# A fused attention and gated-MLP block on one core: the first stage written out as one order of steps, with the first chunk's maxima in it

## The chip, the core and the metric

The kernel runs on one core of a Trainium2 chip. The metric is the device time of one execution in microseconds (us). The core has five engines that run side by side, each working through its own instructions in order: TensorE (PE; its weight loads are listed apart as PEld), VectorE (DVE), ScalarE (ACT), GpSimd (POOL) and SyncE (SP). SP does nothing here but issue DMAs: it too works in order, so a DMA that has to wait for something holds up all DMAs behind it on SP. A few DMAs are issued by POOL instead.

## The reference

From one input of 2048 rows by 512 columns the kernel computes a parallel sum: the input, plus multi-head attention with 32 heads of width 16, plus a gated MLP with a matrix product along the sequence. Both branches read the same layer-normed input.

```python
x = A_x
xn = _layernorm(x, axis=-1)
return x + _A_ref(xn, A_wqkv, A_wo) + _B_ref(xn, B_w_in, B_w_sp, B_b_sp, B_w_out)

# _A_ref: q, k, v = split(x @ wqkv); softmax(q k^T / 4) v, heads joined; @ wo
# _B_ref: z = gelu(x @ w_in); z1, z2 = halves, z2 layer-normed
#         g = w_sp @ z2 + b_sp;  (z1 * g) @ w_out
```

## The kernel before

**Numbers.** Every product but scores, maxima and values is made of three passes over operands that are split into a rounded high part and a low part (`mm3` L242, `split` L238: ACT copies the high part out of PSUM, DVE subtracts it from PSUM to give the low part). Weights that come from memory are split the same way.

**First stage (L1034 to L1078, a fixed order of instructions).** The rows come in four groups g = 0..3 of 512 rows. For each group: `norm_x` takes the mean and variance of each 128-row tile on DVE (L339, L340), the root on ACT (L342), two small operations on DVE (L343, L344), and the scaling of the tile on POOL (L348). `turn_x` transposes the group on PE (L354, four chunks c of 128 columns) and splits each chunk into `xnT[g, c]`. `qk_first` computes q and k of the first eight heads for the group (24 products of 512 columns, L243 to L245), splits them, stores them through SP to memory (`qscr`, `kscr`: two DMAs each, 512 KB and 256 KB), and `load_stacks` reads the rows of the first two heads back into `qst[0]`, `kst[0]` (four DMAs of 96 KB, issued by SP after the stores have landed). V is made in tiles of 128 rows: the first four (EARLY = 4) here, by `v_tile`, between the q and k of the groups. The first two weight pieces (`wqk0`) are loaded twice: by SP as they are, and by POOL's queue rounded to the high part (L260), so that DVE only subtracts (L266). V's weights are split on POOL (L268, L269). The transposed groups 0 and 1 are stored to memory from POOL's queue (L162, eight DMAs of 512 KB).

**Steady stage (from L1079).** Here a planner in Python writes the order. It holds modelled times of PE, ACT, DVE and POOL in `T`, and at each step emits one of:
- S, a score tile (L1149: two products, then one exp of 128x1024 on ACT);
- M, a maximum tile (L1163: two products, then one maximum over 128x1024 on DVE, L868). Sixteen of them give the 512 query rows of one chunk (for two heads); `max_fin` joins them on DVE (L879 to L885), sends them through memory (`mscr`) into two rows of `qst`, and only then the chunk's scores can start (`maxready`);
- D, one dense slot (L1208: two products on the two halves of the array, 0.23 us of PE): all the rest, in a fixed queue: the other twelve V tiles (`v_rest`, 144 slots), q and k of the other heads (288), the MLP's parts, the two output products;
- V, a burst of 32 value products (L1246), which needs the exps of eight S, and, in the first two bursts, the V tiles of rows 0 to 1023 and 1024 to 2047;
- a filler (L1222), products of zeros while nothing else can run.

One cycle is 8 S, 9 or 7 M in turn, up to 24 D and one V (`ORDER`); there are 16 pairs of heads, four chunks each, two cycles a chunk: 128 cycles. A dense unit is 24 slots (18 for the attention's output product), after which its two PSUM banks `dps` are copied out (`yield "e"`, then `"q"`). If a unit ends after more than 11 slots of a cycle, the dense queue is held until that cycle's V (`hold`), so units and cycles keep step. `mx_ok` lets M start at planner time 7.0 (FIRST), and at most 30 of them run ahead before the first scores (LEAD).

## Time and profile before

| | us |
|---|---|
| median of 3 runs | 1860.66 |
| lowest and highest run | 1859.05, 1863.14 |
| the profiled execution | 1862.6 |
| its span, first to last instruction | 1860.4 |
| PE busy | 1811.4 (97%) |
| DVE busy | 1441.5 (77%) |
| ACT busy | 1189.1 (64%) |
| POOL busy | 722.3 (39%) |
| DMA | 306 MB, mean 165 GB/s |

All times below are us from the start of the span. A row of the **timeline** is: start, length, engine, line of the kernel, operation, what it writes `<-` what it reads, partitions x elements, count, and in brackets how long the engine sat idle before it and what ended that. `SPq` is a DMA issue on SP; its start is when SP got to issue it. A row of the **windows** view is a stretch, its length, the busy time of each engine (and how many instructions touch the stretch), PE's granted clock (1.00 is 2.4 GHz, 0.50 is 1.2 GHz), the DMA engines' share and GB/s; where only one line is asked for, only that line's busy time stands. A row of the **groups** view is line, engine, operation, shapes, count | total busy us, mean ns of one | idle time before. Products are pipelined: a row of PE of 0.39 us is followed by the next after 0.23.

### The profile page before, as it was taken

Reading aid. Unit: us, or ns where it says so; the run is one execution under the profiler, and the core shown is the slowest. Engines: PE = TensorE matmul, PEld = TensorE weight load, DVE = VectorE, ACT = ScalarE, POOL = GpSimd, SP = SyncE. Lnnn points to the kernel's source line nnn. Section 1 sums busy time; section 2 is a strip of 40 time slices with the busy share of each in tenths; the row PEclk is TensorE's granted clock in tenths of the full one; section 3 lists DMA queues with packets and bytes.
Section 4 is the critical chain, followed back from the end, with each engine's and each line's share of the span. In section 5 each row is a group of like instructions: output and inputs, shape, how many; then the busy total and the mean of one; then the engine's idle time right before and its main releaser. Section 6 shows DMA issues by size and latency. Waiting matters only on the chain.

```text
span 1860.4 us, 38081 instructions
## 1 busy us (share of the span) xinstructions
PE 1811.4 (97%) x14804; PEld 1099.5 (59%) x14804; DVE 1441.5 (77%) x1677; ACT 1189.1 (64%) x1292; POOL 722.3 (39%) x808
## 2 busy tenths in 40 slices
...
GB/s 227 283 98 282 277 242 87 127 92 110 136 215 134 106 113 204 156 156 162 217 166 199 157 179 206 158 150 155 193 168 182 174 185 143 129 182 149 112 78 90
DMA packets 212124, 306.14 MB, mean 165 GB/s; under 512 B 36816, under 2 KB 108048, under 8 KB 209056
## 3 DMA queue, kind: packets, MB, share of 16 engines
...
q8 instruction: 116, 1.90, 0.4%
...
## 4 chain that ended last, share of the span: by engine, by line
PE 84%; DVE 6%; DMA 4%; POOL 3%; issue 2%; ACT 1%; SPq 1%; DVEq 0%; POOLq 0%; ACTq 0%
PE dps L1208 34%; PE sl L1246 23%; PE sl L1149 13%; PE sl L1163 12%; DVE mm L868 4%; PE dps L1222 1%; DMA zs<-z2scr 1%; DMA kscr<-qkhl 1%; SPq L132 1%; ACT pf L76 1%; POOL wsp L291 1%; DMA wsp_15r<-in_w_spT 0%; POOL wsp L289 0%; DMA wsp_0r<-in_w_spT 0%; DMA qst<-mscr 0%
## 5 line engine op out<-in xcount | busy, mean ns | idle before, releaser
L868 DVE TENSOR_REDUCE mm<-sl 128x2 f32<-128x1024 f32 x1024 | 1224.4, 1222 | 203.7 <-PE sl L1163 199.1
L76 ACT ACTIVATE pf<-sl 128x1024 f32<-128x1024 f32 x1024 | 1041.1, 1026 | 338.8 <-PE sl L1149 297.3
L1246 PE MATMUL sl<-pf,vall 128*32 128x512 f32 x4096 | 468.4, 598 | 0.7 <-DVE mm L868 0.4
L1149 PE MATMUL sl<-qst,kst 50*128 50x512 f32 x2048 | 437.8, 419 | 11.1 <-DVE mm L868 4.3
L1163 PE MATMUL sl<-kst,qst 48*128 48x512 f32 x2048 | 424.0, 406 | 4.5 <-DVE mm L868 2.2
L1208 PE MATMUL dps<-wsp,zs 64*128 64x512 f32 x2352 | 382.1, 393 | 2.6 <-DMA zs<-z2scr 2.6
L1149 PEld LDWEIGHTS sl<-qst,kst 50*128 50x128 f32 x2048 | 195.8, 184 | 218.4 <-issue 79.3
L1246 PEld LDWEIGHTS sl<-pf,vall 128*32 128x32 f32 x4096 | 120.5, 110 | 271.2 <-issue 237.4
L1163 PEld LDWEIGHTS sl<-kst,qst 48*128 48x128 f32 x2048 | 196.5, 185 | 105.9 <-ACT pf L76 55.3
L1208 PEld LDWEIGHTS dps<-wsp,zs 64*128 64x128 f32 x2352 | 229.3, 187 | 40.4 <-DMA zs<-z2scr 4.1
L76 ACT ACTIVATE e<-sl 128x512 f32<-128x512 f32 x64 | 38.3, 598 | 208.0 <-PE sl L1246 198.0
L1266 DVE TENSOR_TENSOR e<-sl,e 128x512 f32<-128x512 f32 x64 | 44.3, 692 | 136.4 <-PE sl L1246 70.2
L774 POOL TENSOR_TENSOR hhl<-z1i,hhl 128x512 fp32r<-128x512 f32 x28 | 35.9, 1292 | 275.8 <-ACT hhl L76 275.8
L1208 PE MATMUL dps<-w,xt 64*128 64x448 f32 x768 | 110.6, 368 | 1.5
L1208 PE MATMUL dps<-wout,hp 64*128 64x512 f32 x672 | 110.3, 392 | 0.0
L915 POOL TENSOR_TENSOR ob<-ob 128x512 f32<-128x512 f32 (+1 forms) x16 | 20.5, 1284 | 201.5 <-DMA ob<-rscr 186.6
L1208 PEld LDWEIGHTS dps<-w,xt 64*128 64x128 f32 x768 | 73.9, 186 | 16.0 <-issue 7.8
L1208 PEld LDWEIGHTS dps<-wout,hp 64*128 64x128 f32 x672 | 65.5, 187 | 9.1
L911 POOL TENSOR_TENSOR ob<-ob 128x512 f32<-128x512 f32 (+1 forms) x16 | 21.0, 1315 | 117.5 <-DMA ob<-escr 117.5
L441 POOL TENSOR_TENSOR qkhl<-qr,qkhl 128x512 fp32r<-128x512 f32 x24 | 30.4, 1286 | 69.9 <-ACT qkhl L76 65.8
L1208 PE MATMUL dps<-wf,zs 64*128 64x512 f32 x336 | 55.5, 392 | 0.1
L1208 PE MATMUL dps<-xnT,wqk 64*128 64x512 f32 x288 | 47.7, 395 | 1.1 <-ACT vall L76 0.4
...
## 6 DMA issues: line engine op xcount, KB each, us to landing
zs<-z2scr SPq DMA_DIRECT2D x192, 256.0 KB
...
```

What stands on the lines that cost most here:

```text
L76: return nc.scalar.activation(out, in_, func, **kw)
L132: nc.sync.dma_start(raw(dst), raw(src))
L441: nc.gpsimd.tensor_sub(hl[:, 1, :], raw_, hl[:, 0, :].bitcast(F32))
L774: nc.gpsimd.tensor_sub(hl[:, 1, :], z1, hl[:, 0, :].bitcast(F32))
L868: nc.vector.tensor_reduce(mmax[g][:, :, t, kc], sl[k], AX.X, ALU.max)
L911: nc.gpsimd.tensor_add(both_[rows, 0, :], both_[rows, 0, :], both_[rows, 1, :])
L915: nc.gpsimd.tensor_mul(both_[rows, 0, :], both_[rows, 0, :], both_[rows, 1, :])
L1149: nc.tensor.matmul(sl[k][:, j, :], kst[p % 2][rows, kt * P:(kt + 1) * P], qst[p % 2][rows, c * 512:(c + 1) * 512], start=True, stop=True)
L1163: nc.tensor.matmul(sl[k][:, j, :], qst[p % 2][rows, tt * P:(tt + 1) * P], kst[p % 2][rows, kc * 512:(kc + 1) * 512], start=True, stop=True)
L1208: nc.tensor.matmul(dps[:, bank, :w], lhs, rhs, start=go, stop=stop)
L1246: nc.tensor.matmul(sl[k][cols:cols + VW, 0, :], vpack(kt + r, 2 * p + j), pf[:, j * 512:(j + 1) * 512], start=n == n_pv, stop=n == n_pv + ...
L1266: nc.vector.tensor_add(e, sl[k][:, 0, :], e)
```

## The change

The first stage becomes one written order. `STEPS` is a string of words, `First.step` emits each word's instructions, and so it fixes the order on each engine; digits are group and chunk (or half, or tile), `*` picks another engine. S: statistics of two tiles, R: root and the small operations, N: scaling (`*`: the second tile on ACT), T: transposes, E: split of a chunk, Q: the twelve products of q (second digit 0) or k (1), F: its split and store (`*`: ACT copies twice and POOL subtracts), L: load back into the stacks, Z: store of a transposed chunk, now on SP, VH and VL: high and low parts of V's weights (`*`: POOL; else ACT and DVE), V and VE: a V tile and its copy, WH and WL: high and low parts of the first weights (ACT, DVE), B: the bias row, M and X: a maximum tile of the first chunk (first digit the 512 keys, second the tile of queries) and its maximum on DVE.

- All sixteen maxima of the first chunk stand in it, so the planner starts with `n_mx = 16` and with `max_fin(0)` at once; FIRST goes.
- The four early V tiles stand behind nearly all q and k.
- 22 idle products (`WARM`) on zeros are put in front of PE's work.
- POOL's second load of the first weights goes; ACT rounds them.
- The store of ones (`cscr`) moves behind the last load of x, the memsets of V's ones move to the front of POOL.
- In the steady stage: `v_out` copies bank 1 on DVE instead of ACT, the hold needs more than 8 slots instead of 11 and is off until all V tiles are done, the planner starts with ACT at 0.6 and DVE at 2.0.

```diff
-FIRST = 7.0
...
+WARM = 22
+STEPS = (
+    "S00 S01 R00 WH0 N00 WL0 R01 S10 N01* T01 S11 WH1 T03 E03 T00 E01 R10 T02 WL1 E02 E00 R11 N10 N11* Q00 T13 T12 "
+    "T11 F00* S20 VH1* S21 E13 R21 E12 Q01 Z13 VH3* T10 N21* S30 R20 E11 E10 Q11 VL1* R30 N20 F01* B VH0 Z03 N30* "
+    "T20 S31 E20 R31 T23 Z02 Z11 L0 F11 Z10 Z01 E23 N31* Q10 F10 T32 T21 T22 T30 E32 E22 E21 Q20 VH2 L1 T31 VL3 E30 "
+    "T33 Q21 VL0 F20 E31 VL2 M02 E33 M00 Q31 X02 F21 M13 M10 L2 X00 Q30 X13 F31 M03 M01 X10 X03 F30 V3 M22 M12 Z00 "
+    "X01 M23 VE3 X22 Z12 V0 VE0 X12 M21 X23 M20 X21 L3 M11 V1 X20 M32 M30 X11 M31 X32 X31 VE1 V2 X30 M33 X33 VE2 "
+)
...
     def v_out(t, bank):
-        yield "A", ta(512)
-        act(vhead[:, t, :, :DH], dps[:, bank, :].rearrange("p (h d) -> p h d", d=DH), AF.Copy)
+        src = dps[:, bank, :].rearrange("p (h d) -> p h d", d=DH)
+        if bank:
+            yield "D", td(512)
+            nc.vector.tensor_copy(vhead[:, t, :, :DH], src)
+        else:
+            yield "A", ta(512)
+            act(vhead[:, t, :, :DH], src, AF.Copy)
         rel()
...
+    class First:
+
+        def __init__(self, w0r, w0, wvr, wv, braw):
+            self.w0r, self.w0, self.wvr, self.wv, self.braw = w0r, w0, wvr, wv, braw
+            self.acc, self.rs, self.mv, self.came, self.split_, self.turn = {}, {}, {}, [], [], 0
+
+        def step(self, word):
+            name = word.rstrip("*0123456789").lower()
+            getattr(self, name)(*map(int, word[len(name):].rstrip("*")), other=word.endswith("*"))
+
+        def take(self, *key):
+            self.turn += 1
+            self.acc[key] = (dps, *sl)[self.turn % 4]
+            return self.acc[key]
+
+        def s(self, g, h, other):
+            self.mv[g, h] = mv = sm.tile([P, 2, 2], F32, tag="mv", name=f"mv{g}_{h}", bufs=4)
+            for i in range(2):
+                st = sm.tile([P, 6], F32, tag="bst", name=f"bst{g}_{h}_{i}", bufs=4)
+                nc.vector.bn_stats(st, xs[g, 2 * h + i])
+                nc.vector.bn_aggr(mv[:, i, :], st)
+
+        def r(self, g, h, other):
+            mv = self.mv[g, h]
+            self.rs[g, h] = rs = sm.tile([P, 2, 2], F32, tag="rs", name=f"rs{g}_{h}", bufs=4)
+            nc.scalar.activation(rs[:, 0, :], mv[:, :, 1], AF.Sqrt, bias=epst)
+            nc.vector.reciprocal(rs[:, 0, :], rs[:, 0, :])
+            nc.vector.scalar_tensor_tensor(rs[:, 1, :], mv[:, :, 0], -1.0, rs[:, 0, :], ALU.mult, ALU.mult)
+
+        def n(self, g, h, other):
+            rs = self.rs[g, h]
+            for i in range(2):
+                x = xs[g, 2 * h + i]
+                if i and other:
+                    act(x, x, AF.Identity, bias=rs[:, 1, i:i + 1], scale=rs[:, 0, i:i + 1])
+                else:
+                    nc.gpsimd.tensor_scalar(x, x, rs[:, 0, i:i + 1], rs[:, 1, i:i + 1], ALU.mult, ALU.add)
+
+        def t(self, g, c, other):
+            acc = self.take("t", g, c)
+            for i in range(4):
+                nc.tensor.transpose(acc[:, 0, i * P:(i + 1) * P], xs[g, i][:, c * P:(c + 1) * P], ident)
+
+        def e(self, g, c, other):
+            xnT[g, c] = t = piece(f"xnT{g}_{c}")
+            split(t[:, 0, :], t[:, 1, :], self.acc["t", g, c][:, 0, :])
+            self.came.append((g, c))
+
+        def z(self, g, c, other):
+            move(xscr[g][c], xnT[g, c])
+
+        def wh(self, a, other):
+            act(self.w0[a][:, 0, :], self.w0r[a], AF.Copy)
+
+        def wl(self, a, other):
+            nc.vector.tensor_sub(self.w0[a][:, 1, :], self.w0r[a], self.w0[a][:, 0, :].bitcast(F32))
+
+        def q(self, g, a, other):
+            acc = self.take("q", g, a)
+            cs = [c for h, c in self.came if h == g]
+            for c in cs:
+                t, w = xnT[g, c], self.w0[a]
+                mm3(acc[:, 0, :], w[:, 0, c * P:(c + 1) * P], w[:, 1, c * P:(c + 1) * P], t[:, 0, :], t[:, 1, :], c == cs[0], c == cs[-1])
+
+        def f(self, g, a, other):
+            acc = self.acc["q", g, a][:, 0, :]
+            hl = hilo(f"qkhl0_{a}_{g}")
+            if other:
+                raw_ = t512(f"qr0_{a}_{g}")
+                act(raw_, acc, AF.Copy)
+                act(hl[:, 0, :], raw_, AF.Copy)
+                nc.gpsimd.tensor_sub(hl[:, 1, :], raw_, hl[:, 0, :].bitcast(F32))
+            else:
+                split(hl[:, 0, :], hl[:, 1, :], acc)
+            qk_store((qscr, kscr)[a][0], QK[a], hl, slice(g * 512, (g + 1) * 512), True)
+
+        def l(self, g, other):
+            load_stacks(0, slice(g * 512, (g + 1) * 512))
+
+        def b(self, other):
+            bhl = hilo("bhl")[0:16, :, 0:P]
+            nc.vector.tensor_copy(bhl[:, 0, :], self.braw)
+            nc.vector.tensor_sub(bhl[:, 1, :], self.braw, bhl[:, 0, :].bitcast(F32))
+            for a in range(2):
+                move(bsplit[a:a + 1, :], bhl[:, a, :])
+
+        def vh(self, c, other):
+            t, rw = self.wv[c], self.wvr[c]
+            if other:
+                nc.gpsimd.tensor_copy(t[:, 0, :], rw)
+            else:
+                act(t[:, 0, :], rw, AF.Copy)
+
+        def vl(self, c, other):
+            t, rw = self.wv[c], self.wvr[c]
+            (nc.gpsimd if other else nc.vector).tensor_sub(t[:, 1, :], rw, t[:, 0, :].bitcast(F32))
+            self.split_.append(c)
+
+        def v(self, t, other):
+            acc = self.take("v", t)
+            rows = slice((t % 4) * P, (t % 4 + 1) * P)
+            cs = self.split_
+            for c in cs:
+                x, w = xnT[t // 4, c], self.wv[c]
+                mm3(acc[:, 0, :], x[:, 0, rows], x[:, 1, rows], w[:, 0, :], w[:, 1, :], c == cs[0], c == cs[-1])
+
+        def ve(self, t, other):
+            act(vhead[:, t, :, :DH], self.acc["v", t][:, 0, :].rearrange("p (h d) -> p h d", d=DH), AF.Copy)
+
+        def m(self, kc, t, other):
+            acc = self.take("m", kc, t)
+            for j in range(2):
+                rows = slice(64 * j, 64 * j + KS)
+                nc.tensor.matmul(acc[:, j, :], qst[0][rows, t * P:(t + 1) * P], kst[0][rows, kc * 512:(kc + 1) * 512], start=True, stop=True)
+
+        def x(self, kc, t, other):
+            if 0 not in mmax:
+                mmax[0] = at_.tile([P, 2, 4, 4], F32, tag="mm", name="mm0", bufs=2)
+            nc.vector.tensor_reduce(mmax[0][:, :, t, kc], self.acc["m", kc, t], AX.X, ALU.max)
+
...
         load_x(0)
+        w0r = [begin(*qk_weights(0, a)) for a in range(2)]
         w0 = [piece(f"wqk0_{a}") for a in range(2)]
-        w0r = [begin(*qk_weights(0, a), early=w0[a]) for a in range(2)]
         load_x(1)
         load_x(2)
         ones = t512("ones")
         nc.vector.memset(ones[0:32, 0:P], 1.0)
-        move(cscr.rearrange("o (a b) -> (o a) b", b=P), ones[0:16, 0:P])
+        for r in (0, 64):
+            nc.vector.tensor_copy(onesr[r:r + 2, :], ones[0:2, 0:P])
+        nc.gpsimd.memset(vhead[:, :, :, DH:], 1.0)
+        nc.gpsimd.memset(vall[:, NT * H * (DH + 1):], 0.0)
         wv = [(qst, kst)[c // 2][1].rearrange("p (b a f) -> p b a f", b=2, a=2)[:, c % 2] for c in range(ND)]
         wvr = [begin(f"wv{c}", wqkv[c * P:(c + 1) * P, 2 * D:3 * D], 512) for c in range(ND)]
         load_x(3)
+        move(cscr.rearrange("o (a b) -> (o a) b", b=P), ones[0:16, 0:P])
         braw = t512("braw")[0:16, 0:P]
-        bhl = hilo("bhl")[0:16, :, 0:P]
         move(braw, b_sp)
         init_rows(0, move)
-        for r in (0, 64):
-            nc.vector.tensor_copy(onesr[r:r + 2, :], ones[0:2, 0:P])
-        run(norm_x(0, 2))
-        turn_x(0)
-        for r, t in zip(w0r, w0):
-            end(r, t, True)
-        run(norm_x(1, 2))
-        nc.gpsimd.memset(vhead[:, :, :, DH:], 1.0)
-        nc.gpsimd.memset(vall[:, NT * H * (DH + 1):], 0.0)
-        for g in range(NG):
-            run(qk_first(g, w0))
-            load_stacks(0, slice(g * 512, (g + 1) * 512))
-            if g == 0:
-                nc.vector.tensor_copy(bhl[:, 0, :], braw)
-                nc.vector.tensor_sub(bhl[:, 1, :], braw, bhl[:, 0, :].bitcast(F32))
-                for a in range(2):
-                    move(bsplit[a:a + 1, :], bhl[:, a, :])
-            if g + 1 < NG:
-                turn_x(g + 1)
-            if g + 2 < NG:
-                run(norm_x(g + 2, 2))
-            if g == 0:
-                for r, t in zip(wvr, wv):
-                    end(r, t)
-            for t in ((), (0,), (1, 2), (3,))[g]:
-                v_tile(t, wv)
-            if g in (1, 2):
-                for c in range(ND):
-                    store(xscr[g - 1][c], xnT[g - 1, c])
+        for _ in range(WARM):
+            nc.tensor.matmul(dps[:, 1, :], zeror, brow, start=True, stop=True)
+        first = First(w0r, w0, wvr, wv, braw)
+        for word in STEPS.split():
+            first.step(word)
         steady.append(True)
-        T.update(P=0.0, A=0.0, D=0.0, G=0.0)
+        T.update(P=0.0, A=0.6, D=2.0, G=0.0)
...
-        n_st = n_mx = n_pv = 0
+        spawn(max_fin(0), 0, T["D"])
+        n_st, n_mx, n_pv = 0, 16, 0
...
-            return n_mx < LEAD and t > FIRST
+            return n_mx < LEAD
...
-                    hold = spent > 11 and n_pv < N
+                    hold = spent > 8 and n_pv < N and len(vdone) == NT - EARLY
```

## Rows read from the trace of the kernel before

**Rows 1.** Windows view, all engines, two stretches: PE, PEld, DVE, ACT, POOL busy
```profile
0.00:64.50 64.50, 49.16 (x208) 37.31 (x208) 34.22 (x83) 18.47 (x36) 27.79 (x44) 0.97 0.75 258
...
146.30:1793.50 1647.20, 1628.28 (x13523) 980.60 (x13521) 1316.69 (x1494) 1103.58 (x1179) 662.50 (x727) 1.00 0.60 164
```

**Rows 2.** Windows view of the dense slots alone (L1208), single cycles
```profile
130.80:146.30 15.50, 8.03 (x52) 1.00 0.49 164
159.60:173.40 13.80, 8.13 (x48) 1.00 1.03 311
407.40:420.80 13.40, 0.00 (x0) 1.00 0.29 86
1765.20:1779.30 14.10, 3.30 (x20) 1.00 0.34 100
1822.20:1833.70 11.50, 5.13 (x38) 1.00 0.25 93
1833.70:1844.30 10.60, 0.00 (x0) 1.00 0.00 0
```

**Rows 3.** Timeline of PE: end of the first stage, first score, first burst
```profile
65.36 1.66 PE L1208 MATMUL dps<-qst,xnT 64*128 64x512 f32 x12 [0.69 <-ACT vall L76]
...
74.64 0.49 PE L1163 MATMUL sl<-kst,qst 48*128 48x512 f32 x1 [0.33 <-DMA kst<-kscr]
...
103.92 0.40 PE L1149 MATMUL sl<-qst,kst 50*128 50x512 f32 x2
...
115.96 3.64 PE L1246 MATMUL sl<-pf,vall 128*32 128x512 f32 x32
```

**Rows 4.** Timeline of DVE: the first maxima and the end of `max_fin`
```profile
71.77 5.79 DVE L868 TENSOR_REDUCE mm<-sl 128x2 f32<-128x1024 f32 x5 [8.41 <-PE sl L1163]
...
92.69 0.21 DVE L885 STREAM_TRANSPOSE ms<-mrow 128x32 f32<-128x32 f32 x1
```

**Rows 5.** Groups view, 0 to 64.5 us: operations of DVE and POOL
```profile
L339 DVE BATCH_NORM_STATS2 bst<-x 128x6 f32<-128x512 f32 x16 | 10.8, 672 | 2.6 <-DMA x<-in_x 2.6
L240 DVE TENSOR_TENSOR xnT<-sl,xnT 128x512 fp32r<-128x512 f32 x12 | 7.8, 682 | 4.4 <-ACT xnT L76 4.4
...
L340 DVE BATCH_NORM_AGGREGATE mv<-bst 128x2 f32<-128x6 f32 x16 | 2.9, 182 | 0.6
...
L348 POOL TENSOR_SCALAR x<-x,rs 128x512 f32<-128x512 f32 x16 | 12.2, 768 | 20.3 <-DVE rs L344 12.2 <-DMA x<-in_x 8.1
L269 POOL TENSOR_TENSOR kst<-wv3r,kst 128x512 fp32r<-128x512 f32 x1 | 1.3, 1280 | 0.1
```

**Rows 6.** Timeline of SP: stores of q and k, and loads after them
```profile
22.17 0.90 SPq L132 DMA_DIRECT2D qscr<-qkhl  x2
...
25.81 0.77 SPq L132 DMA_DIRECT2D qst<-qscr  x1
...
50.14 1.79 SPq L132 DMA_DIRECT2D kscr<-qkhl  x2
...
61.60 0.32 SPq L132 DMA_DIRECT2D kst<-kscr  x1
...
71.79 0.41 SPq L132 DMA_DIRECT2D kst<-kscr  x1
```

**Rows 7.** Windows view: a stretch with the DMA queues full
```profile
50.00:52.00 2.00, 1.85 (x10) 1.46 (x10) 2.00 (x5) 1.46 (x3) 0.00 (x0) 1.00 1.01 373
```

**Rows 8.** Timelines of DVE and POOL: one small operation, alone and beside POOL
```profile
32.20 0.16 DVE L344 SCALAR_TENSOR_TENSOR rs<-mv,rs 128x2 f32<-128x2 f32 x1
...
39.74 0.55 DVE L344 SCALAR_TENSOR_TENSOR rs<-mv,rs 128x2 f32<-128x2 f32 x1
...
39.66 0.61 POOL L268 CAST kst<-wv3r 128x512 fp32r<-128x512 f32 x1
```

**Rows 9.** Windows view of the maximum products alone (L1163)
```profile
64.50:116.00 51.50, 14.00 (x70) 1.00 0.43 149
```

**Rows 10.** Timeline of ACT: copy of the last two of the twelve V tiles
```profile
121.26 1.08 ACT L76 ACTIVATE vall<-dps 128x512 f32<-128x512 f32 x2
```

65 lines of the change are left out of this document (2 added, 63 removed).

## The prediction

> **What bounds the kernel now.** I read the busy times by stage first. From 146.3 to 1793.5 PE works 1628 of 1647 us; in the first 64.5 us it is busy 49 (much of it at half clock or waiting inside), DVE 34 [rows 1]. That suggests that PE's work sets the time, so the next view was the dense slots cycle by cycle [rows 2]. It says otherwise: 13.8 us with 24 slots (48 products), 13.4 with none, 14.1 with 10. The cycle of 8 S, 8 M and a burst takes about 13.5 us whether or not its dense room is full. There are 128 cycles, so the end is the moment the cycles get going plus 128 cycles, as long as the dense queue ends in time. It does, with a little room: cycle 121 (1765.2) holds 10 slots and cycle 126 (1833.7) none.
>
> So the stage that counts is the one up to the first bursts. PE's timeline [rows 3]: the first stage ends on PE at 65.36 - 0.69 = 64.7 (T0), the first score is at 103.92, the first burst at 115.96; the second is at 130.8 and the third at 146.3 [rows 2]. Between T0 and the first score DVE waits 8.41 us for maxima to begin at 71.77, does 16 of them at 1.16 us, and the joined maxima leave it at 92.9 [rows 4]; the score comes 11.0 after. In that time PE runs dense slots, so the 39 us are not idle; what counts is how much work is left at each point.
>
> **The change, part by part.** All times are of the profiled execution (1862.6, span 1860.4).
>
> *DVE's floor.* DVE has 34.2 us of work in the first stage [rows 1], about 32 of it after the first x is in at 4.6. Added: three VL (0.68 each) and 16 maxima (1.16 each, 18.6); removed: two low parts that go to POOL (1.4). That is 4.6 + 32 + 2.0 - 1.4 + 18.6 = 55.8 if DVE never waits. PE's last product (M33) runs before the last maxima, some 1.7 us earlier: T0 would be 54. I expect DVE to wait, for the stacks.
>
> *The stores and loads on SP.* SP issues in order, so I walk its words from F01. F01's low part is on POOL behind N20, which needs R20 on DVE. Ahead of R20 stand seven S (1.7 each: 2 x (0.67 + 0.18)), five R (0.36), two WL and six E (0.62 to 0.68 each) [rows 5]: 11.9 + 1.8 + 1.3 + 3.7 after 4.6 is 23.3, R20 itself 23.6, two scalings of 0.77 make 25.2, the subtraction of 1.28 makes 26.5. A lone store lands 3.6 us after its issue (22.17 to 25.81), about 1.5 after its data; a load is usable 2.85 after its last issue (71.79 to 74.64) [rows 3, 6]. With the queues full 373 GB/s move [rows 7]; so F (786 KB) takes 2.0 to 2.1 us, Z (524 KB) 1.4, L (393 KB) 1.0. Issues cost SP 0.45 each.
> - F01 issued 26.5 to 27.4, B to 28.3, three Z to 29.6, L0 waits for F01's landing at 30.2, to 31.7; F11 to 32.6, Z10 and Z01 to 33.5, F10 to 34.4. The data queue behind them: F01 until 29.3, three Z 33.4, L0 34.4, F11 36.4, two Z 39.1, F10 41.1, landed 42.6. L1 therefore goes out at 42.6 to 44.2, and M13 and M10 (second key chunk) can run at about 46.7; PE would be there at about 40.6.
> - F20 and F21 are ready (DVE 35 and 39.5) but stand behind L1: issued to 46.0, data to 49, landed 50.5; L2 to 52.2, usable 54.7.
> - Q30 stands behind M13 on PE: 47.1 to 49.8, its low part 52.2. F31 and F30 are issued to 53.8, data to 57.3, landed 58.8; L3 to 60.4, usable 62.9.
> - M32 at 62.9, four maxima of 1.18 after it to 67.9, and M33 on PE behind V2 (12 products, 2.7 us) at 66. **T0 = 66.**
> Each leg has bounds: the quickest store in the trace took 3.6 us from issue to landing, the slowest 11.5 (50.14 to 61.60, with eight Z of POOL in the queues) [rows 6]. All three legs at the quickest fall under DVE's own pace, with T0 between 54 and 58; all at 11.5 give about 78.
>
> *Idle products.* 22 products of 512 columns on zeros can start when POOL has cleared them, near 2; at half clock they take 9.4 us and would reach 11.4, when the fourth tile of x is scaled (10.7). Cost 0 to 0.3, since the first E waits for DVE's S11 (12.7) anyway. Their gain, full clock for Q00, is also hidden: Q00 ends with the last E of the group on DVE (16.1). I take 0.
>
> *First weights by ACT.* Two copies of 0.6 us on ACT, which is idle then; 512 KB less to load in front brings x3 1.3 us forward, where S30 has three to spare. 0. *Scaling on ACT* is not in the trace: from a copy (0.54 each [rows 10]) to POOL's 0.77, off DVE's path: 0. *`cscr`* behind x3 makes SP wait until about 20 for the four row loads behind it; F00 is ready near 19.7. 0. If x3 came 2 us later it would cost that.
>
> *DVE beside POOL.* The small operation L344 took 0.16 alone and 0.55 when it began inside a POOL cast, ending with it [rows 8]. WL, VL and the eight R on DVE read two operands from SBUF while POOL is busier than before; 2 of 8 were held 0.4 to 0.5 us. Some 13 such operations, each held between 0 and a POOL operation (1.28): 0 to 5 us; I take 1 on the path to F01. **T0 = 67.** The Trainium skill says why in "SBUF — State Buffer" (section SBUF: two separate sides): DVE and GpSimd share one pair of ports as an exclusive lock for a whole instruction, if DVE reads two operands there. The trace agrees (0.55 beside 0.16). By the rule alone every one of the 13 could wait a full POOL operation, and T0 would be 71.
>
> *From T0 to the third burst.* The second burst needs V tiles up to 15, so all 144 slots of `v_rest`. Before, these took from 64.7 to 122.3 [rows 3, 10] beside 35 M by 116 [rows 9] and 2 after, 11 S and a burst: 192 x 0.233 + 3.6 = 48.3 of 57.6, so 9.3 of gaps (0.7 at each copy of the banks). After: 25 M (9 while the maxima travel, then 9 and 7 of ORDER), 16 S, a burst: 185 x 0.233 + 3.6 = 46.7. Gaps 7.8, as DVE copies one bank while ACT copies the other and nothing waits for the last stack. The second burst is at T0 + 54.5. The first score, ready 11 to 12 after T0, isn't what is late. Units then start in step with cycles, so the third burst follows after 13.8 [rows 2] (15.5 before): **T0 + 68.3 = 135.3 against 146.3, 11.0 earlier.** The break-even is T0 = 78.
>
> *The dense queue.* At the third burst 168 slots are done, against 192: one unit late. Cycles 121 and 126 have room for it: 0; if not absorbed, a unit in the last but one cycle costs 11.5 - 10.6 = 0.9 [rows 2]. The hold at 8 instead of 11 changes nothing where units of 24 are in step: 0, up to one cycle's misfit (1.7, as 15.5 against 13.8).
>
> Sum: 1862.6 - 11.0 = 1851.6 for an execution like the profiled one; the median of before stands 1.9 lower, so **1849.7, say 1850**.
>
> **The rivals.**
> - *The stacks come early and DVE alone sets T0* (legs near 3.6): T0 54 to 58, the third burst 20 to 24 earlier: 1837 to 1841. For it: lone stores do land in 3.6. Against: F11 and F10 share the queue with five Z.
> - *The stacks come as late as the slowest row* (11.5 on each leg): T0 = 78, nothing left: 1861. For it: that row exists. Against: eight Z of a second queue were in front of it.
> - *The dense queue sets the end* (slower). If the end is its last slot, what counts is when slot 168 is done: before at about 131 (24 slots, a cycle of 15.5, ahead of the third burst), after at 135.3, 4 later: 1865. For it: PE is busy 1628 of 1647 us [rows 1], and nearly all cycles hold dense work. Against: the cycles with 10 and with no slots. It decides if those rooms are gone and T0 is past 63.
> - *The change doesn't do what it says*: the written order stalls on one engine's head and the maxima still trickle in after the V tiles. That is T0 near 74 and a time near 1857.
>
> **How the numbers follow.** Forecast (T0 62 to 72, 1844 to 1855) 0.48; early stacks 0.24; stall in the order 0.11; slowest legs 0.08; dense queue 0.09. About 0.2% (3.7 us) is what a measurement can tell from no change: faster is below 1857, so all of the first two and half of the stall: 0.78; same 0.13 (the slowest legs and the other half); slower 0.09. The range leaves out the dense queue and half of the slowest legs above and a little of the early stacks below: 1838 to 1860. A cycle that waits for memory costs some 4 us either way, which lies inside it.
>
> **What would show it.** PE: last first-stage product at 62 to 72, M13 near 47, M32 near 63, both ended by DMA of `kst`. SP: L1 issued near 43, L2 near 51, L3 near 59. First score about 12 after T0, second burst at T0 + 54. Cycles 117 to 125 without fillers while attention's output waits. Wrong would be: maxima back to back on DVE (early stacks), cycles of more than 14 us in a row, or dense slots left after the last burst.

## The result: 0.35% slower, and the profile after

The changed kernel takes 1868.55 us (median of 20 runs, 1860.84 to 1872.04) against 1861.12 for the kernel before (20 runs, 1857.67 to 1865.63): a ratio of 1.0035, 95% interval 1.0026 to 1.0043. The profiled execution has a span of 1867.0 us against 1860.4. The forecast was 1850, faster, with a range of 1838 to 1860; the direction was wrong.

I call the stretch from the start of one burst to the start of the next a cycle, and count from 0, as the prediction does. Where did the 6.6 us of the spans come from? Cycle 4 begins at 166.0 instead of 173.4, so the start did win 7.4 us; what follows takes 1701.0 instead of 1687.0, 14.0 more. Windows view of the kernel after, all engines (start:end, length, then busy time of PE, PEld, DVE, ACT, POOL, granted clock, DMA share, GB/s), the stretches of [rows 1]:

```profile
0.00:68.00 68.00, 58.21 (x268) 42.61 (x268) 52.04 (x100) 25.54 (x48) 18.86 (x29) 0.97 0.79 279
138.40:1799.80 1661.40, 1635.75 (x13544) 987.92 (x13543) 1319.33 (x1499) 1105.77 (x1182) 667.69 (x733) 0.99 0.59 163
```

The first stage does what it was written for: DVE is busy for 52 us of 68 and no longer waits 8.41 us for the first maxima [rows 4]. Timeline of PE after, the rows that answer to [rows 3]:

```profile
45.53 0.46 PE L1081 MATMUL sl<-kst,qst 48*128 48x512 f32 x1 [3.91 <-DMA kst<-kscr]
...
67.18 0.93 PE L1204 MATMUL sl<-kst,qst 48*128 48x512 f32 x6
...
80.60 0.40 PE L1190 MATMUL sl<-qst,kst 50*128 50x512 f32 x2
...
94.05 3.64 PE L1287 MATMUL sl<-pf,vall 128*32 128x512 f32 x32
```

The first product of the planner's part is at 67.18 (T0), the first score at 80.60 (before 103.92), the first burst at 94.05 (115.96). The second burst is at 124.57 (130.8), the third at 138.4 (146.3). From there the lead is lost in a few single cycles. Windows view of the dense slots after (L1249), as in [rows 2]: cycle 8, a normal one, and five long ones:

```profile
220.10:233.40 13.30, 7.80 (x48) 4.55 (x48) 1.00 0.93 324
233.40:252.70 19.30, 10.25 (x48) 6.95 (x48) 0.91 0.86 253
559.70:578.00 18.30, 8.98 (x48) 5.25 (x48) 0.91 0.63 189
606.70:623.40 16.70, 6.71 (x30) 4.12 (x30) 0.80 0.17 64
745.20:761.20 16.00, 8.37 (x48) 5.10 (x48) 1.00 0.63 190
1351.60:1369.30 17.70, 10.58 (x48) 6.78 (x48) 0.90 0.90 196
```

These are cycles 9, 32, 35, 45 and 90; the same cycles before took 13.8, 13.9, 13.9, 13.4 and 12.9. They cost 20 us together. Cycles 75, 88 and 123, which were long before (18.3, 15.1, 17.1), are shorter now and give 8 back. The dense slots of before (L1208) in cycles 9 and 32:

```profile
241.80:255.60 13.80, 8.12 (x48) 4.67 (x48) 1.00 0.87 302
561.60:575.50 13.90, 7.87 (x50) 4.64 (x48) 1.00 0.75 188
```

Cycle 37 divides the loss. Windows of the dense slots, cycles 4 to 36 and then 37 to the end, after and before:

```profile
166.00:636.70 470.70, 226.69 (x1440) 143.22 (x1440) 0.99 0.51 156
636.70:1867.00 1230.30, 682.21 (x4204) 409.58 (x4204) 1.00 0.61 161
```

```profile
173.40:629.90 456.50, 230.22 (x1488) 144.17 (x1488) 1.00 0.53 160
629.90:1860.40 1230.50, 666.59 (x4108) 399.60 (x4108) 1.00 0.60 159
```

All 14 us are lost up to cycle 36: 5.6 in cycle 9, 4.4 in 32, 1.4 in 34 and 2.8 in 35. From cycle 37 on the two kernels take the same time; there 45 and 90 are paid for by 75, 88 and 123.

What PE waited for in two of them. Cycle 9, timelines of SP and then of PE:

```profile
222.59 1.16 SPq L139 DMA_DIRECT2D mscr<-ms  x1
223.85 0.40 SPq L139 DMA_DIRECT2D xnT__2413<-xscr  x1
...
231.80 0.32 SPq L139 DMA_DIRECT2D xnT__2471<-xscr  x1
233.00 1.97 SPq L139 DMA_DIRECT2D qst<-mscr  x2
...
240.47 1.10 PE L1190 MATMUL sl<-qst,kst 50*128 50x512 f32 x2 [3.48 <-DMA qst<-mscr]
```

The joined maxima leave at 222.59 and are back in `qst` at 240.4, nearly 18 us later; between them on SP stand four loads of a transposed group (512 KB each), stores of q and k and loads of the stacks. The products that follow run at a lower clock: the granted clock is 0.69 from 240.5 to 246, partly the level of 1.2 GHz and partly that of 2.4, so that a wait of 3.5 costs 5.6. Windows view, all engines:

```profile
240.50:246.00 5.50, 5.42 (x31) 4.14 (x32) 2.47 (x3) 2.83 (x3) 0.00 (x0) 0.69 0.99 212
```

Cycle 32, timelines of ACT and PE:

```profile
566.35 0.63 ACT L83 ACTIVATE z1u<-z1u 128x512 f32<-128x512 f32 x1 [6.73 <-POOL z1u L562]
566.89 0.58 ACT L83 ACTIVATE e<-sl 128x512 f32<-128x512 f32 x1
...
567.52 0.50 PE L1190 MATMUL sl<-qst,kst 50*128 50x512 f32 x2 [2.54 <-ACT e L83]
```

ACT works in order: it stands 6.73 us at a tanh of the MLP whose input POOL has not finished, and the copy of `e`, which frees the bank that the next score needs, stands behind it. ACT makes this copy at the first burst of each chunk only (L1302 of the kernel after; at the second DVE adds, L1307), so in every second cycle.

### The profile page after: what moved, and what is told of

It reads as the page before. It is cut to its first block, busy times and chain, and to the rows that moved or that the text cites. A ratio compares the mean times of both kernels' runs of the same rounds, so it can differ in the third digit from the quotient of the medians.

```text
span 1867.0 us, 38081 instructions
## 1 busy us (share of the span) xinstructions
PE 1816.6 (97%) x14808; PEld 1103.5 (59%) x14808; DVE 1447.1 (78%) x1684; ACT 1194.5 (64%) x1297; POOL 710.7 (38%) x790
## 4 chain that ended last, share of the span: by engine, by line
PE 84%; DVE 5%; POOL 4%; DMA 3%; issue 2%; ACT 1%; SPq 0%; DVEq 0%; POOLq 0%; ACTq 0%
PE dps L1249 34%; PE sl L1287 22%; PE sl L1190 13%; PE sl L1204 12%; DVE mm L808 3%; DMA qst<-mscr 1%; PE dps L1263 1%; DMA qscr<-qkhl 1%; ACT pf L83 1%; POOL wsp L276 1%; DVE bst L987 1%; POOL wsp L274 0%; SPq L139 0%; POOL z2hl L492 0%; POOL z L490 0%
## 5 line engine op out<-in xcount | busy, mean ns | idle before, releaser
L808 DVE TENSOR_REDUCE mm<-sl 128x2 f32<-128x1024 f32 x1008 | 1208.2, 1222 | 206.6 <-PE sl L1204 202.0
L1204 PE MATMUL sl<-kst,qst 48*128 48x512 f32 x2016 | 419.6, 407 | 5.3 <-DVE mm L808 3.1
L1249 PE MATMUL dps<-wsp,zs 64*128 64x512 f32 x2352 | 381.9, 393 | 2.2 <-DMA zs<-z2scr 2.2
L1204 PEld LDWEIGHTS sl<-kst,qst 48*128 48x128 f32 x2016 | 194.1, 186 | 106.2 <-ACT pf L83 53.9
L1249 PEld LDWEIGHTS dps<-wsp,zs 64*128 64x128 f32 x2352 | 229.6, 187 | 38.6 <-DMA zs<-z2scr 2.9
L1307 DVE TENSOR_TENSOR e<-sl,e 128x512 f32<-128x512 f32 x64 | 44.2, 691 | 130.8 <-PE sl L1287 64.0
L1249 PE MATMUL dps<-w,xt 64*128 64x448 f32 x768 | 110.8, 368 | 1.5
L1249 PE MATMUL dps<-wout,hp 64*128 64x512 f32 x672 | 109.8, 392 | 0.0
L1249 PEld LDWEIGHTS dps<-w,xt 64*128 64x128 f32 x768 | 74.1, 186 | 15.8 <-issue 7.7
L1249 PEld LDWEIGHTS dps<-wout,hp 64*128 64x128 f32 x672 | 65.3, 187 | 9.6
L1249 PE MATMUL dps<-wf,zs 64*128 64x512 f32 x336 | 55.9, 393 | 0.1
L1249 PE MATMUL dps<-xnT,wqk 64*128 64x512 f32 x288 | 48.3, 394 | 0.3
```

The source lines that it names most:

```text
L808: nc.vector.tensor_reduce(mmax[g][:, :, t, kc], sl[k], AX.X, ALU.max)
L1204: nc.tensor.matmul(sl[k][:, j, :], qst[p % 2][rows, tt * P:(tt + 1) * P], kst[p % 2][rows, kc * 512:(kc + 1) * 512], start=True, stop=True)
L1249: nc.tensor.matmul(dps[:, bank, :w], lhs, rhs, start=go, stop=stop)
L1307: nc.vector.tensor_add(e, sl[k][:, 0, :], e)
```

## The experiments

Theory **phase**: the start's gain is real, but it shifts the dense queue by one unit against the cycles. A chunk is two cycles long, and in one of the two its maxima travel through memory and ACT copies `e`. Moved by one cycle, other parts of the dense work, with their stores, loads and evacuations, fall beside these. Rivals: **total work** (the last dense slot sets the end, wherever it waits on the way), **planner edits** (the copies on DVE, the hold, the start values) and the new first stage itself.

Lag is how many cycles later than in the kernel before a dense unit comes; the changed kernel has a lag of 1. With the hold above 8 slots this is so up to cycle 36 only. There a unit that was cut in two ends after 9 slots and is held, so the queue falls back by one more unit, and from cycle 37 on the changed kernel has the same dense products in the same cycles as a_lag2 and b_lag2 (read from the traces' operands, cycle by cycle). All results in one place (ratio to the kernel before in the same set of runs):

| kernel | first stage | lag | median us | ratio, 95% interval |
|---|---|---|---|---|
| b_lag1 | old | 1 | 1881.8 | 1.0122 (1.0101 to 1.0144) |
| b_lag2 | old | 2 | 1855.0 | 0.9958 (0.9947 to 0.9970) |
| a_lag0 | new | 0 | 1871.1 | 1.0059 (1.0044 to 1.0074) |
| changed kernel | new | 1 | 1868.6 | 1.0035 (1.0026 to 1.0043) |
| a_lag2 | new | 2 | 1855.1 | 0.9968 (0.9954 to 0.9982) |
| a_lag3 | new | 3 | 1873.9 | 1.0069 (1.0049 to 1.0090) |
| a_vact | new | 1 | 1864.5 | 1.0014 (1.0000 to 1.0027) |
| a_oldplan | new | 1 | 1881.5 | 1.0097 (1.0067 to 1.0127) |
| a_hold11 | new | 1 | 1882.8 | 1.0115 (1.0096 to 1.0133) |
| a_mq | new | 1 | 1878.1 | 1.0084 (1.0060 to 1.0109) |
| a_fetch | new | 1 | 1858.4 | 0.9985 (0.9975 to 0.9996) |
| a_tanh | new | 1 | 1863.8 | 1.0016 (1.0004 to 1.0028) |
| a_both | new | 1 | 1857.1 | 0.9979 (0.9967 to 0.9990) |
| b_odd | old | 1 | 1861.4 | 1.0004 (0.9995 to 1.0013) |
| a_fetch_b | new | 1 | 1859.2 | 0.9991 (0.9982 to 1.0000) |
| a_lag2_b | new | 2 | 1854.8 | 0.9968 (0.9956 to 0.9980) |
| b_lag2_b | old | 2 | 1854.5 | 0.9967 (0.9955 to 0.9979) |
| a_rest1 | new | 2 | 1853.9 | 0.9966 (0.9952 to 0.9979) |
| a_rest3 | new | 2 | 1853.4 | 0.9965 (0.9954 to 0.9976) |

### The dense queue's lag alone

The edit for one more unit of lag, in `has_dense`, is a rest of the dense queue behind the third burst (`n_pv` goes up by 8 with each burst, so 24 to 31 is cycle 2); with 40 for 32 it is two units:

```diff
             nonlocal blocked, swap, hold, seen
+            if 24 <= n_pv < 32 and not slots:
+                return False
             while not slots:
```

b_lag1 is the kernel before with it:

> The kernel before, with its dense queue resting in the cycles between the fourth and the fifth burst of 8 value products (n_pv 24 to 31): from there on every dense unit comes one cycle later, as it does in the changed kernel, while the first stage is untouched. Theory 'phase' (one unit of lag puts the dense queue's copies, stores and loads beside the maxima's trip through memory, and single cycles of 15 to 19 us appear near cycles 9, 32, 35 and 45): 5 to 14 us slower than before, 1866 to 1875. Theory 'total work' (the end is the last dense slot, wherever the rest lies): about one cycle's dense work pushed back, 0 to 6 slower, 1861 to 1867, with no new long cycles. Theory 'planner edits' (copy of bank 1 on DVE and the new hold make the long cycles): as before, 1861.

It took 1881.8, 21 us more, with no change of the first stage. Windows view of its dense slots (L1210), cycles 9 and 32:

```profile
240.20:258.90 18.70, 10.28 (x48) 7.06 (x48) 0.91 0.86 259
565.40:584.50 19.10, 8.97 (x48) 5.25 (x48) 0.91 0.67 181
```

The same two long cycles as in the changed kernel, from the lag alone. PE waited there for the same things, `qst<-mscr` and ACT's `e` (3.3). It was more than expected; most of the rest is in cycles 36 to 39, which a_hold11 explains.

a_lag0 takes the lag away from the changed kernel: the second burst waits for a seventh dense unit, and the hold is off until then.

```diff
                 elif it[0] == "q":
-                    hold = spent > 8 and n_pv < N and len(vdone) == NT - EARLY
+                    udone[0] += 1
+                    hold = spent > 8 and n_pv < N and udone[0] > 6
...
-            elif op == "V" and ... for k in range(n_pv, n_pv + CYC) if EARLY <= k < NT):
+            elif op == "V" and ... if EARLY <= k < NT) and (not n_pv or udone[0] > 6):
```

> The changed kernel, in which the second burst waits for a seventh dense unit (the first unit of the next q and k), and units are not held until then: the dense queue then stands to the cycles as in the kernel before, and some 6 us of the 8 that the first stage won by the third burst are given back at once. Theory 'phase': no long cycles near 9, 32, 35 and 45; third burst some 2 us earlier than before and the end 1 to 3 us earlier than before: 1857 to 1860, 8 to 11 us faster than the changed kernel. Theory 'total work': the dense queue is where it was at each time, so no more than 2 us from the changed kernel, 1866 to 1870. Theory 'planner edits': the long cycles stay, 1866 to 1872.

Half of it came true. The long cycles are gone; its windows view of the dense slots (L1251), cycles 1, 9 and 32:

```profile
135.60:150.10 14.50, 7.62 (x48) 4.66 (x48) 1.00 0.53 182
246.60:260.40 13.80, 8.15 (x48) 4.71 (x48) 1.00 0.79 276
567.00:580.90 13.90, 7.90 (x50) 4.56 (x48) 1.00 0.88 207
```

But the time is 1871.1, not 1857 to 1860. With the dense queue at the same place as before, the second burst comes at 135.6 instead of 130.8: measured by the dense queue the new start is 4.8 us later, not earlier. What it wins in bursts it takes from the dense queue. The span ends 6.8 later.

a_lag2 is the changed kernel with one rest, b_lag2 the kernel before with two:

> The changed kernel, with its dense queue resting in one more cycle (n_pv 24 to 31), so that it is two units behind the kernel before. Chunks change every second cycle, so if what counts is whether a unit ends in the first or the second cycle of a chunk ('phase' by parity), the long cycles go again and the time is 1856 to 1862. If more lag is simply worse ('phase' by distance), the long cycles stay or grow: 1868 to 1880. Theory 'total work': the end moves by the dense work pushed back, 1868 to 1875, without long cycles of a new kind.

> The kernel before, with its dense queue resting for two cycles (n_pv 24 to 39), so that it is two units behind where it was, as in the changed kernel with one rest. One rest made it 21 us slower, with cycles of 18.7 and 19.1 at 9 and 32. Theory 'parity' (a unit that falls into the other cycle of its chunk collides; two units put it back): the cycles at 9 and 32 are 13.8 and about 14 again and the time is 1856 to 1862; and then the changed kernel with one rest, 1855.1 (profiled 1852.4), differs from it only by the start, 7 us in the profiles. Theory 'distance' (each unit of lag costs): more than 1882. If it comes out near 1852, two units of lag are what gains, and the new first stage gains nothing.

Both are faster than the kernel before: 1855.1 and 1855.0, by 0.3 to 0.4%, a little more than either forecast. Windows view of the dense slots of a_lag2 (cycles 9 and 32), then of b_lag2 (L1210, the same):

```profile
235.50:249.40 13.90, 8.21 (x48) 4.75 (x48) 1.00 0.85 310
553.40:567.60 14.20, 4.84 (x28) 2.60 (x28) 1.00 0.39 117
```

```profile
238.10:252.30 14.20, 8.13 (x48) 4.70 (x48) 1.00 0.87 322
555.70:570.00 14.30, 4.85 (x28) 2.60 (x28) 1.00 0.39 116
```

Two units of lag put the long cycles right again, with either first stage: parity, not distance. Cycles 4 to 36 take 456.6 and 455.5 us, as before (456.5), and not 470.7; behind them the changed kernel does the same dense work in the same cycles, so its odd lag costs what it costs up to there. That b_lag2 equals a_lag2 was named in its forecast as the case in which the new first stage gains nothing; see the last part of this section.

> The changed kernel, with its dense queue resting for two cycles (n_pv 24 to 39): three units behind the kernel before. Theory 'parity': the long cycles at 9 and 32 are back (18 to 21 each) and the time is 1865 to 1880. Theory 'distance, the other way' (a later dense queue is simply better, whatever its parity): 1848 to 1856, until its last units come after the last burst. The last three units of attention's output have room for two, so up to one cycle, 11 us, may come on top at the end in either case.

It took 1873.9. ACT's wait is back, two cycles on: cycle 34 takes 18.3 with PE waiting 2.7 for `e`. Cycle 9 is not: it takes 14.1, and cycle 11 takes 14.8. The last unit no longer fits either, and the last cycle, with 36 slots in it, takes 23.8 instead of 16.1. So parity holds for the collision on ACT; of the one in cycle 9, made of loads that stay in place by time and loads that move with the queue, it is not the whole account.

### The planner edits

```diff
-        src = dps[:, bank, :].rearrange("p (h d) -> p h d", d=DH)
-        if bank:
-            yield "D", td(512)
-            nc.vector.tensor_copy(vhead[:, t, :, :DH], src)
-        else:
-            yield "A", ta(512)
-            act(vhead[:, t, :, :DH], src, AF.Copy)
+        yield "A", ta(512)
+        act(vhead[:, t, :, :DH], dps[:, bank, :].rearrange("p (h d) -> p h d", d=DH), AF.Copy)
```

> The changed kernel, with both banks of a V pair copied by ACT, as before (v_out without the DVE branch). The gaps of 1.41, 0.96 and 0.47 us in front of V's slots that end with DVE's copy shrink to about 0.7: second burst 1 to 3 us earlier. Theory 'phase': the rest is as in the changed kernel, 1864 to 1869. Theory 'planner edits' with this edit as the cause: the long cycles go, 1856 to 1861.

It took 1864.5. Waits view of PE from 67 to 125, the changed kernel and then a_vact (waited for: us in total, times, longest):

```profile
PE dps L1249 <- DVE vall L420: 4.3, 4, 1.4
```

```profile
PE dps L1244 <- ACT vall L83: 3.1, 3, 1.2
```

The waits shrink by 1.2 us, yet its second burst is at 124.6 too (124.57), and cycles 9 and 32 take 21.1 and 19.9. The copies are not the cause of the long cycles. The 4 us between this kernel and the changed one stand, in the profiles, behind cycle 37, where the two have the same dense work (1226.3 against 1230.3); no run explains them.

a_oldplan undoes the other planner edits as well (hold above 11, start values 0):

> The changed kernel with all the planner edits of the steady stage undone as far as they can be: both banks of a V pair copied by ACT, the hold above 11 slots instead of 8, the planner's ACT and DVE starting at 0 instead of 0.6 and 2.0 (the hold stays off until the V tiles are done). Theory 'phase': the dense queue stands where it stands in the changed kernel, so the long cycles at 9, 32 and 45 are there: 1863 to 1870. Theory 'planner edits': they are gone and the time is 1848 to 1856.

It took 1881.5, slower by far, against every theory. a_hold11 undoes the hold alone:

```diff
-                    hold = spent > 8 and n_pv < N and len(vdone) == NT - EARLY
+                    hold = spent > 11 and n_pv < N and len(vdone) == NT - EARLY
```

> The changed kernel with the hold above 11 slots, as before, instead of 8 (still off until the V tiles are done). The order of instructions then has 27 dense slots in each of cycles 36, 37 and 38, where the changed kernel has 9, 24 and 24. In the kernel before with one rest the same three cycles of 27 slots and the one after took 15.1, 15.9, 15.0 and 15.4. If the hold is worth nothing (the prediction's 0), 1866 to 1870; by those cycles, 1.5 to 2 us each and the dense lag that follows, 6 to 13 us slower than the changed kernel: 1875 to 1882.

It took 1882.8: the hold at 8 is worth 14 us of the changed kernel. Windows view of the dense slots (L1249) of a_hold11, cycles 36 to 39:

```profile
627.50:642.60 15.10, 8.33 (x54) 5.05 (x54) 1.00 0.40 125
642.60:658.50 15.90, 8.44 (x56) 4.95 (x54) 1.00 0.31 101
658.50:673.50 15.00, 8.52 (x56) 5.27 (x54) 1.00 0.06 20
673.50:689.00 15.50, 7.58 (x50) 4.69 (x48) 1.00 0.76 205
```

Cycle 35 ends with a unit cut in two (15 slots, then 9). Nine is not over 11, so nothing is held and three cycles of 27 slots follow, 61.5 us for the four; the changed kernel holds at 9 and takes 54.2. From then on its units are split otherwise too, and 37 to the end takes 1242.0 instead of 1230.3. The same cycles are long in b_lag1 and a_oldplan, which also hold above 11. So the planner edits saved the changed kernel from a worse end.

### The two collisions

a_mq sends the maxima over POOL's queue instead of SP's:

```diff
+    def move_p(dst, src):
+        nc.gpsimd.dma_start(raw(dst), raw(src))
...
-        after(0.3, move, mscr[g % 4]...
+        after(0.3, move_p, mscr[g % 4]...
-            after(6.5 if g else 3.3, move, qst...
+            after(6.5 if g else 3.3, move_p, qst...
```

> The changed kernel, in which the joined maxima travel on POOL's queue: mscr<-ms and qst<-mscr are issued by GpSimd, everything else as it was on SP. In cycle 9 of the changed kernel the first score waited 3.48 us for qst<-mscr, 4 KB that SP issued at 233.0, 10.4 after mscr<-ms, behind four loads of xnT, q and k stores and stack loads. If that queue is the cause, cycle 9 falls from 19.4 to 13.8 to 15, and the wait of 1.9 in cycle 45 goes too, while cycle 32 (ACT behind POOL) and cycle 90 (load of zs) stay: 6 to 8 us faster than the changed kernel, 1860 to 1863. If POOL, whose own instructions are up to 1.3 to 2.1 us each, issues them later than SP did, new waits of qst<-mscr show in other cycles: 1868 or more.

It took 1878.1, and cycle 9 takes 19.3, as in the changed kernel. The issues view of this kernel (KB each, median us from issue to landing), then the tile view of `mscr` from 215 to 250 us, then its windows, all engines:

```profile
qst<-mscr POOLq DMA_DIRECT2D x128, 4.0 KB, 2.3
mscr<-ms POOLq DMA_DIRECT2D x64, 16.0 KB, 3.0
```

```profile
DMA to landing us min/median/max: 7.4/7.8/7.9
```

```profile
228.00:234.00 6.00, 5.92 (x50) 4.42 (x48) 4.99 (x5) 4.68 (x5) 0.74 (x2) 1.00 1.00 328
234.00:241.00 7.00, 3.80 (x34) 1.04 (x32) 2.52 (x3) 2.55 (x4) 3.01 (x3) 1.00 1.05 325
```

On a queue of its own each leg of the trip took 7.4 to 7.9 us instead of 2.3 and 3.0, while the DMA engines were busy all the time (share 1.00). In all, from the issue of `mscr<-ms` to the first score, it took 15.9 us (225.26 to 241.16) instead of 17.9. But POOL, with subtractions of its own in front, issued it 1.9 us later against the start of cycle 9, and PE's wait stayed (3.37 instead of 3.48). So the order on SP makes up some 2 us of the trip, and this run alone doesn't rule it out as a part of the cause; the slow legs come from the traffic. The other trips of this kernel say the same: worked out from its trace, a leg during which the engines' share was under 0.3 landed after 1.8 (`mscr<-ms`, median of 12) or 2.0 us (`qst<-mscr`, 65), with a share of 0.95 or more after 7.4 (8) or 7.8 (6). The Trainium skill, "DMA: Bandwidth & Descriptors" (Queues, rings and completion order), says that a DMA engine goes round between its queues and drains a whole packet of one, typically some 9 to 17 descriptors (single pieces of a transfer), before it switches. By that a queue of its own needn't let a small transfer pass at once; how long such a turn was, no run here shows. The kernel is 9.5 us slower than the changed one; the largest wait that PE has more is for `zs<-z2scr`, 7.4 instead of 2.2.

a_fetch takes the traffic away instead: two of the fetches of a transposed group are made a cycle later.

```diff
-                if m == 2 and g in (3, 0):
+                if m == 3 and g in (3, 0):
                     fetch_xnT((g + 1) % NG, 0.5)
```

> The changed kernel, in which the second and fourth fetch of a transposed group (4 loads of 512 KB) are made one dense unit, so one cycle, later: those of cycle 8 (223.85 to 231.80) move out of the maxima's trip through memory into cycle 9, and those of cycle 5 move into the trip of cycle 6. All else is in the same order. When the trip was put on another queue it still took 8.0 and 7.4 us a leg while the DMA engines were 100% busy. If the traffic beside the trip makes cycle 9 long, cycle 9 falls from 19.4 to 13.8 to 16 and cycle 7 may grow by up to as much (there are no stores of rounded weights beside that trip): 0 to 6 us faster than the changed kernel, 1862 to 1868. If the four loads don't matter, cycle 9 stays at 19 to 20.

It took 1858.4, 10 us faster than the changed kernel, more than the 0 to 6 expected, and faster than the kernel before. Timeline of SP, then windows of the dense slots (L1249) for cycles 9 and 32, then of all engines during the trip:

```profile
223.01 0.38 SPq L139 DMA_DIRECT2D mscr<-ms  x1
229.53 2.03 SPq L139 DMA_DIRECT2D qst<-mscr  x2
232.64 0.36 SPq L139 DMA_DIRECT2D xnT__2554<-xscr  x1
```

```profile
233.90:247.70 13.80, 8.14 (x48) 4.67 (x48) 1.00 1.03 294
554.20:573.50 19.30, 8.76 (x48) 5.21 (x48) 0.91 0.60 178
```

```profile
223.00:240.00 17.00, 16.91 (x147) 10.15 (x138) 12.16 (x12) 12.15 (x14) 5.83 (x5) 1.00 1.00 271
```

Cycle 9 takes 13.8, cycle 7 doesn't grow (13.8), cycle 32 stays. That settles cycle 9: the four loads beside the trip. The second leg goes out 6.5 us behind the first instead of 10.4. The DMA engines' share is 1.00 here too, so the share by itself doesn't tell a trip that is in time from one that is late; what the edit changed is how much is queued beside it. Cycle 9 is 5.6 of the 10 us. The rest isn't explained: in the profiles it lies in cycles 35, 45, 90 and 124 (14.0 and 13.9 in 35 and 45), where the dense work is the same, and 35 and 45 vary between two profiles of this one kernel.

a_tanh makes the planner place the tanh later:

```diff
+        yield "T", 4.2
         yield "A", ta(512)
         act(u, u, AF.Tanh, scale=GC)
```

> The changed kernel, in which the planner puts the tanh of the gate (z1u on ScalarE) at least 4.2 us later than POOL's modelled end. In cycle 32 of the changed kernel ACT stood 6.73 us at the head of its queue for POOL's z1u, with the copy of e, which frees a score's bank, and the exps behind it; PE then waited 2.54. If that in-order wait makes cycle 32 long, it falls from 18.3 to 14 or 15, and the kernel is about 4 us faster than the changed kernel, 1863 to 1866. If POOL's own backlog is the limit, the wait comes back at another instruction and cycles 32 to 36 together stay as long (76 to 78 us): 1867 to 1872. The dense units per cycle stay as they are but for cycles 35 and 36 (10 and 14 slots instead of 15 and 9).

It took 1863.8. Timeline of ACT:

```profile
562.57 0.60 ACT L83 ACTIVATE e<-sl 128x512 f32<-128x512 f32 x1 [3.80 <-PE sl L1288]
...
573.98 0.63 ACT L83 ACTIVATE z1u<-z1u 128x512 f32<-128x512 f32 x1
```

The copy of `e` no longer stands behind a tanh, and cycle 32 takes 13.6; cycles 32 to 36 take 72.5 instead of 77.0. That settles cycle 32.

a_both has both edits:

> Both edits together, later fetches and later tanh. If the two collisions are what the odd unit of lag costs, the changed kernel with both keeps most of what its first stage gained: 1856 to 1861, no more than 1 us from the kernel before. If they only move elsewhere, 1866 to 1872.

It took 1857.1: within the range, 11 us faster than the changed kernel and 4 faster than the kernel before. It adds little to a_fetch; cycles 35, 45 and 90 took 16.3, 14.8 and 18.5 in it. Its cycles 4 to 36 take 460.5 us, against 470.7 in the changed kernel and 455.5 to 457.9 in the kernels with a lag of 0 or 2: the two collisions are 10 of the 14 us, and cycles 34 and 35 are the others.

### What the new first stage is worth

b_odd is the old first stage with the same dense units per cycle as a_fetch from the fourth cycle on (but for two slots that stand in cycle 22 instead of 21): b_lag1 with the hold above 8 and the later fetches.

> The kernel before with one rest of its dense queue (n_pv 24 to 31), the hold above 8 slots instead of 11, and the second and fourth fetch of a transposed group one dense unit later. From the fourth cycle on its dense units fall into the same cycles as in the changed kernel with the later fetches (1858.4); only the first stage and the copies of V differ. If the new first stage is worth what its third burst says (146.3 against 138.4 to 139.5, less one rest of some 1 us that is shorter than a full cycle): 5 to 7 us slower than that kernel, 1863 to 1866. If it is worth nothing in the end, 1857 to 1860. By the hold and the fetch, 16 to 24 us faster than with the rest alone (1881.8).

It took 1861.4, between its two forecasts. Three kernels were run again beside it:

> The changed kernel with the later fetches once more, beside the same kernel with the old first stage: 1855 to 1860. The difference of the two is what the new first stage is worth where the dense queue stands one unit behind: 5 to 7 us if the gain at the third burst stays, 0 if something later takes it.

> The changed kernel with one rest once more, beside the old first stage with two rests: 1852 to 1857. In the profiles its fourth cycle began 3.5 us earlier and its last one 1.5. If that is the first stage's worth at two units of lag, it is 1 to 4 us faster than the other.

> The kernel before with two rests once more: 1853 to 1857; 1 to 4 us slower than the changed kernel with one rest if the first stage's gain lasts, the same within 1 us if it doesn't.

At a lag of 1 the new first stage wins 2.1 us (1859.2 against 1861.4; the two intervals overlap by a little), at a lag of 2 nothing (1854.8 against 1854.5). In the profiles of these kernels it leads by 4.6 to 4.8 at the third burst. The 7.9 of the first pair was high: the old first stage had its third burst at 144.2 to 146.4 in five profiles, the new one at 138.4 to 139.7. At a lag of 1 the lead lasts to the end in a_fetch (5.8 ahead of b_odd), while in a_fetch_b cycle 45 takes it (17.1 against 13.9). At a lag of 2 the cycle behind the rest is 17.5 long (15.6 in a_lag2), 3.7 more than a normal one; timeline of PE of a_lag2_b there:

```profile
157.37 0.84 PE L1190 MATMUL sl<-qst,kst 50*128 50x512 f32 x2 [1.79 <-DMA qst<-mscr]
```

a_rest1 and a_rest3 move the rest:

> The changed kernel whose dense queue rests in the cycle behind the second burst (n_pv 16 to 23) instead of the one behind the third; from cycle 4 on its dense units fall into the same cycles as with the rest behind the third burst (1854.8 and 1855.1). There the cycle behind the rest was 15.6 and 17.5 long, 1.8 to 3.7 more than 13.8, with a wait for qst<-mscr of 1.5 to 1.8 beside three stores of rounded weights. If that cycle took the first stage's lead, the fourth cycle begins near 165 instead of 167.3 to 169.4 and the time is 1851 to 1853. If a cycle behind any rest is long, or later cycles take the lead, 1854 to 1857.

> The same with the rest one cycle later than behind the third burst (n_pv 32 to 39). Cycle 3 is then the cycle without dense slots (some 13.4), cycle 2 the full one (13.25): the fifth cycle begins near 178.5 instead of 180.6 and 183. If the lead lasts, 1851 to 1853; if later cycles (45 and 90, which took 15 to 19 in one run and 13 to 17 in another) take it, 1854 to 1857.

They took 1853.9 and 1853.4, between the two forecasts. With the rest elsewhere the lead is 4.4 to 4.6 at cycle 3 and 3.5 at cycle 8, and lasts to cycle 44. Then cycle 45 takes 17.6 and 16.4 instead of 14.2, and cycle 46 begins at 749.3 and 748.3, as with the old first stage (749.0). Timeline of PE of a_rest1:

```profile
737.35 0.68 PE L1190 MATMUL sl<-qst,kst 50*128 50x512 f32 x2 [2.11 <-DMA qst<-mscr]
```

Again the maxima's trip, and one reason can be read from the traces. Windows view of the changed kernel up to its first burst, its 16 written maxima (L1081, two products each) and the planner's (L1204):

```profile
0.00:94.05 94.05, 6.36 (x32) 2.72 (x32) 0.98 0.71 253
```

```profile
0.00:94.05 94.05, 6.79 (x36) 3.33 (x36) 0.98 0.71 253
```

16 and 18 maxima are 34 at the first burst; before it was 35 [rows 9]. The order of a cycle is fixed, so the maxima stay one tile closer to their scores to the end: from the issue of `mscr<-ms` to the first score of its chunk, the median over the chunks is 15.1 us in the changed kernel and in a_rest1, and 16.3 in the kernel before and in b_lag2_b. Each trip has 1.2 us less to hide in. That this is what makes cycle 45 long with the new first stage is argued, not shown: no kernel with one maximum more was run. The lowest median, 1853.4 of a_rest3, is 0.35% below the kernel before. It can't be told from the other kernels with a lag of 2, b_lag2 with the old first stage among them (ratios 0.9958 to 0.9968). Why a lag of 2 is some 6 us better than none was not tried.

## Why the prediction was wrong, point by point

- **The walk along SP was right up to the second key chunk.** L1 was issued at 42.37 (forecast 42.6), M13 ran at 45.53 to 46.56 (46.7), L2 went out at 48.42 (50.5), L3 at 58.06 (58.8), and PE left the first stage at 67.2 (67). The last leg was not what set that. The only waits of PE for `kst` in the first stage are the two at L1 (3.91 and 0.56); M32 ran at 63.00 (62.9) without a wait, behind V1 in PE's order, where the prediction had it ended by the DMA. So the last 20 us came out right by PE's own work, in part by luck.
- **DVE beside POOL** was taken at 1 of 0 to 5 us. Source view of the small operation after (min/median/max ns of one):

```profile
L995 DVE SCALAR_TENSOR_TENSOR rs<-mv,rs x8: 160/160/538, 8.0 to 28.1; 128x2 f32<-128x2 f32 x8
```

  One of the eight was held to 538 ns, as in [rows 8], and another to 0.33 us; the low parts of V's weights took 0.68 and were not held. Half a microsecond in all. By the rule of the Trainium skill that the prediction weighed ("SBUF — State Buffer", SBUF: two separate sides), T0 would have been 71 if every one had waited; it was 67.2.
- **From T0 to the second burst** the gaps were sized at 7.8. It took 57.4 us for the 46.7 of work, so 10.7, and 4.3 of these are waits for the copy by DVE, which I had taken for the quicker way. a_vact, without that copy, has its second burst at 124.6 too, so what fills the gaps otherwise stays open. The third burst came 7.9 earlier instead of 11.0. A term mis-sized by 3.
- **128 cycles of the same length** is the step that failed. From rows of full and empty dense slots [rows 2] I read that the dense queue has room and its place doesn't matter, and put its lag of one unit at 0, or 0.9 at the very end. The lag cost 14.5 us behind the third burst, 14.2 of them in cycles 4 to 36 (470.7 instead of 456.5): not by its amount, but by what falls beside the maxima's trip and beside ACT's copy of `e`. b_lag1 shows it without the first stage, a_fetch and a_tanh take away its two largest parts, and a_lag2 and b_lag2, with one unit more, have 456.6 and 455.5 there. The prediction did say that a cycle that waits for memory costs some 4 us, and took it as scatter of either sign. Here there are three such cycles (9, 45 and 90). The first comes from the odd lag. 45 and 90 belong to the places of the dense work from cycle 37 on, which the kernels with a lag of 2 share: 90 takes 15.0 to 21.1 us in all kernels with these places and 12.9 to 13.4 in all others. That part as a whole takes what it took before.
- **The hold** was put at 0, at most 1.7. With a lag of 1 it is worth 14 us, in the changed kernel's favour (a_hold11). The misfit does not end after one cycle: at a hold above 11, three cycles of 27 slots follow, and the splits after them differ.
- **The rival of the dense queue** named the right side and nearly the size (1865), by a mechanism that this kernel doesn't follow: a_fetch wins 10 us with every dense unit left in its cycle, and b_lag2, with two units of lag, ends earlier than before. But its price was right for what it described: it put the dense queue at the third burst 4 us late, and a_lag0, held to the old places, had its second burst 4.8 late and its end 6.8.
- **How much the start can be worth** was overestimated even with the odd lag's collisions gone: 0 to 2 us of time from 4.7 at the third burst.
